# Up products that stream the high and the low part of x through one load of the high weights

## The chip, the cores and the metric

The kernel runs on one core of a Trainium2 chip. The metric is the device time of one execution in microseconds; before the change it is 268.32 us (median of three runs, 266.75 to 272.85).

## What is computed

A linear-attention recurrence over 768 steps (4 sequences, 8 heads of 48 channels) gives 3072 rows of 384 numbers, out. A mixture of experts then works on these rows: a row whose skip score is positive goes to the one of 8 experts with the largest gate logit.

```
def _moe_ref(x, w_skip, w_gate, w1, w2):
    out = x.copy()
    do_compute = x @ w_skip > 0
    xc = x[do_compute]
    e_idx = np.argmax(xc @ w_gate, axis=1)
    ...
    for e in range(E):                       # E = 8
        mask = e_idx == e
        h = np.maximum(xc[mask] @ w1[e], 0.0)        # up: 384 -> 1024
        y[mask] = gate_w[mask, None] * (h @ w2[e])   # down: 1024 -> 384
    out[do_compute] = xc + y
```

## The kernel before

The first 120 us or so compute the recurrence, write its rows to `out` in device memory, and build per expert a list of at most 232 rows (`CAP`). The change lies in what follows, the experts.

**Precision.** Products are made of numbers of a reduced kind, fp32r. Every operand is split in a high part, which is its rounded value, and a low part, which is what the rounding left. A product is the sum of three: high times high, low times high, high times low.

**Weights.** An expert's w1 and w2 are 6144 columns of 128 rows. They come in 12 pieces of 512 columns (`load_piece`, L106, issued on SP's queue). `split_piece` (L112) makes the parts: L115 on ScalarE casts a piece to its high part, L116 subtracts it from the raw piece, on VectorE or, for every third piece, on GpSimd. The pieces of expert e+1 are split while expert e computes. Raw pieces wait in `NST2` = 14 buffers; each split piece lets the next load start.

**One expert** (`expert`, L1009) works on its 232 rows in this order, which is the order of the instructions on every engine, since the program's order is kept there:

- Up (`up`, L155). The 1024 hidden features are eight slices of 128. A slice takes nine matmuls of 232 columns on TensorE: for each of three chunks of the 384 inputs the high weights with the high x, the high weights with the low x, the low weights with the high x, each with a weight load of its own, all into one PSUM region. Two slices share one PSUM bank; there are four banks of this kind (`banks`, L829: ps_p, ps_r, ps_l, ps_y).
- `rectify` (L163), once for a pair of slices: ScalarE writes the high part of the rectified sum, `hh` (L164), VectorE the low part, `hl` (L165), both straight from PSUM, 464 columns at once.
- `split_next(2)` after each pair splits two pieces of the next expert's weights, eight in the up phase.
- The next expert's rows are transposed (`turn`, L147): six transposes on TensorE, the high part xh on ScalarE (L152), the low part xl on VectorE (L153).
- Down (`down`, L167), for rows 0 to 127 and then 128 to 231: 24 matmuls of 384 columns, three for each slice, in the order of the slices: hh with the high w2, hh with the low w2, hl with the high w2. Two pieces are split behind each half, then `mix` (L173) on VectorE scales by the gate and adds x, and GpSimd scatters the rows to `out` (L178).

Expert 0 is done by other code (`single`), interleaved with the end of the recurrence and with the first two pairs of expert 1. Experts 2 and 3 have a few short VectorE instructions at their start (L1069 to L1086), which look for values out of range.

## Time and profile before

| what | value |
|---|---|
| median of three runs | 268.32 us |
| the profiled execution | 267.35 us |
| its span, from first to last instruction | 265.7 us |
| TensorE busy | 94% of the span |
| VectorE, ScalarE, GpSimd busy | 70%, 53%, 49% |
| experts 1 to 7 (up matmuls of expert 1 to the last mix) | 134.4 to 259.6 us |
| one full expert | 17.1 us |

The prediction shows rows of several views. A row of the chain of waits has a start, a length, the engine, the tile written, the line and a count. A row of a timeline has start, length, engine, line, operation, what is written and read, the sizes, and in brackets how long the engine had been idle and what ended that. A row by source line gives least, median and largest length in ns and the first and last start. In a row by groups stand total busy time, the mean in ns, and the idle time ahead. A window's row has the busy time of each engine. "PEld" are weight loads, which run beside the matmuls. Lines are those of the kernel before.

### The profile page before, as it was taken

The numbers are of one execution on the slowest core, as the hardware profiler recorded it, in microseconds if no ns is written. First come the engines' busy times: TensorE is split into PE (matmuls) and PEld (weight loads), VectorE is DVE, ScalarE is ACT, GpSimd is POOL, SyncE is SP. The second block draws the span as 40 slices with busy tenths as digits, with TensorE's granted clock in tenths as the row PEclk, the third lists the DMA queues.
The fourth block names the chain that finished last, engine by engine and source line by source line (L and its number), as shares of the span: only waits on it lengthen the run. The fifth ranks groups of instructions, "written<-read, shape, count | busy, mean of one in ns | idle before, by whom it ended". The sixth has DMA issues, their size and how long they took to land.

```text
span 265.7 us, 8819 instructions
## 1 busy us (share of the span) xinstructions
PE 249.5 (94%) x3593; PEld 229.1 (86%) x3594; DVE 187.3 (70%) x364; ACT 139.5 (53%) x314; POOL 130.9 (49%) x130
## 2 busy tenths in 40 slices
PE   7899888989999999899999999999999999999990
PEld 2689777877988989778799899999999999999990
DVE  7997446588989989786466996988478385692300
ACT  2556555656757667445377706648176282670200
POOL 8666233353728625502878837455535445345011
PEclk9999999999999999999999999999999999999997
DMA  6968788988899886449599797777738566001000
GB/s 196 292 191 265 210 239 266 275 273 266 246 260 280 238 276 179 104 119 317 164 326 277 248 323 259 219 233 243 251 110 259 171 205 218 20 1 46 0 35 21
DMA packets 31137, 53.92 MB, mean 203 GB/s; under 512 B 4603, under 2 KB 14471, under 8 KB 31088
## 3 DMA queue, kind: packets, MB, share of 16 engines
q1 hardware_dynamic: 28896, 48.09, 60.0%
q0 software_dynamic: 2048, 5.18, 6.2%
q8 instruction: 30, 0.49, 0.8%
q14 instruction: 19, 0.16, 0.2%
q10 hardware_dynamic: 144, 0.00, 0.0%
HBM read 45.46 MB, written 8.39 MB: 203 GB/s over the span
## 4 chain that ended last, share of the span: by engine, by line
PE 71%; DVE 18%; DMA 4%; issue 3%; ACT 1%; SPq 0%; POOL 0%; POOLq 0%; DVEq 0%
PE ps_p L170 11%; PE ps_y L170 11%; PE ps_p L446 6%; PE ps_p L160 5%; PE ps_r L160 5%; PE ps_l L160 5%; PE ps_y L160 5%; PE ps_y L508 5%; DVE am L467 3%; PE ps_s L479 3%; DVE am L468 3%; DVE rd L416 2%; PE ps_l L459 2%; DVE rd L424 2%; PE ps_y L532 2%
## 5 line engine op out<-in xcount | busy, mean ns | idle before, releaser
L116 POOL TENSOR_TENSOR lo<-raw,hi 128x512 fp32r<-128x512 f32 x40 | 54.1, 1355 | 59.7 <-ACT hi L115 48.6
L115 ACT CAST hi<-raw 128x512 fp32r<-128x512 f32 x96 | 54.7, 623 | 0.0
L116 DVE TENSOR_TENSOR lo<-raw,hi 128x512 fp32r<-128x512 f32 x56 | 50.7, 930 | 2.5 <-ACT hi L115 1.9
L434 POOL TENSOR_TENSOR kd<-dm,w_d 128x512 f32<-128x512 f32 x23 | 31.6, 1382 | 15.4 <-DMA dm<-in_dm_dram 8.3
L178 POOL DMA_INDIRECT out_dram<-xg,sid x16 | 17.3, 1079 | 36.3 <-DVE xg L175 28.5
L467 DVE COPY_PREDICATED am<-below,ps_p 128x512 f32<-128x512 int8 x24 | 17.7, 738 | 17.6 <-PE ps_p L446 17.5
L446 PE MATMUL ps_p<-rd,kd 64*64 64x128 f32 x768 | 27.3, 276 | 0.8 <-issue 0.8
L128 POOL DMA_INDIRECT xg<-out_dram,gid x16 | 18.4, 1151 | 16.8 <-DMA raw<-in_w_dram 10.8
L446 PEld LDWEIGHTS ps_p<-rd,kd 64*64 64x64 f32 x768 | 21.0, 132 | 4.5 <-issue 2.4
L508 PE MATMUL ps_y<-vz,am 128*64 128x96 f32 x384 | 20.6, 248 | 3.9 <-DVE am L468 1.6
L164 ACT ACTIVATE hh<-ps_p 128x464 fp32r<-128x464 f32 x7 | 3.9, 559 | 37.6 <-PE ps_p L160 22.9
L410 ACT ACTIVATE rd<-rd,uw 128x128 f32<-128x128 f32 x50 | 17.2, 395 | 9.6 <-DVE rd L416 9.6
L508 PEld LDWEIGHTS ps_y<-vz,am 128*64 128x64 f32 x384 | 17.4, 137 | 5.2 <-ACT xT L576 1.9
L479 PE MATMUL ps_s<-vz,kt 128*64 128x96 f32 x352 | 19.6, 252 | 0.9 <-issue 0.9
L461 ACT COPY kt<-ps_l 128x512 f32<-128x512 f32 x22 | 12.9, 585 | 13.0 <-PE ps_l L459 12.8
L170 PE MATMUL ps_p<-hi,hh 128*128 128x384 f32 x56 | 19.4, 347 | 0.0
L170 PE MATMUL ps_p<-hi,hl 128*128 128x384 f32 x56 | 19.0, 340 | 0.4 <-issue 0.4
L479 PEld LDWEIGHTS ps_s<-vz,kt 128*64 128x64 f32 x352 | 15.3, 136 | 4.3 <-issue 4.2
L170 PE MATMUL ps_y<-hi,hh 128*104 128x384 f32 x56 | 18.9, 338 | 0.0
L170 PE MATMUL ps_y<-lo,hh 128*104 128x384 f32 x56 | 18.9, 337 | 0.0
L170 PE MATMUL ps_y<-hi,hl 128*104 128x384 f32 x56 | 18.9, 337 | 0.0
L170 PE MATMUL ps_p<-lo,hh 128*128 128x384 f32 x56 | 18.8, 336 | 0.0
(239 smaller groups left out, 670.3 us busy)
## 6 DMA issues: line engine op xcount, KB each, us to landing
raw<-in_w_dram SPq DMA_DIRECT2D x96, 256.0 KB
dm<-in_dm_dram SPq DMA_DIRECT2D x24, 512.0 KB
vz<-in_tok_dram SPq DMA_DIRECT2D x48, 96.0 KB
out_dram<-xt SPq DMA_DIRECT2D x48, 96.0 KB
out_dram<-xt SPq DMA_DIRECT2D x4, 192.0 KB
xg<-out_dram,gid POOLq DMA_INDIRECT x16
out_dram<-xg,sid POOLq DMA_INDIRECT x16
wgp<-in_wgq_dram SPq DMA_DIRECT2D x1, 96.0 KB
```

The costliest lines, as they stand in the source:

```text
L115: nc.scalar.copy(hi, t)
L116: eng.tensor_tensor(lo, t, hi.bitcast(F32), ALU.subtract)
L128: ins = nc.gpsimd.indirect_dma_start(out=xg[:m], out_offset=None, in_=out[0:rows], in_offset=bass.IndirectOffsetOnAxis(ap=gid[:m, q : q + ...
L160: nc.tensor.matmul(ph, a[:, c, fs], b[:, c, :], start=(k == 0), stop=(k == 3 * NCC - 1))
L170: nc.tensor.matmul(py, a, b[:, f, :], start=(k == 0), stop=(k == 3 * NFC - 1))
L178: ins = nc.gpsimd.indirect_dma_start(out=out, out_offset=bass.IndirectOffsetOnAxis(ap=sid[: listed(q), q : q + 1], axis=0), in_=xs.pop(q)[ ...
L410: nc.scalar.mul(rd[:, :, 1], rd[:, :, 0], uw[:, hp : hp + 1])
L434: (eng or nc.gpsimd).tensor_tensor(kds[n], d[:, 1], w_d[:, n % NSUB, 1][:, :, None].to_broadcast([DR, NHP, 2, C]), ALU.mult,)
L446: nc.tensor.matmul(ps_p[q * C : (q + 1) * C, a, 2 * hp * C : 2 * (hp + 1) * C], kd[h, hp, q, :], rd[h, hp, q].rearrange("p s c -> p (s c)" ...
L467: nc.vector.copy_predicated(shape(am[n % 2]), below, p[:, :, 0])
L479: nc.tensor.matmul(s[a * C : (a + 1) * C, :, hp * D : (hp + 1) * D], kt[:, hp, a, :], t[:, :, a, hp, :], start=i == 0 and hp == 0, stop=Tr ...
L508: ins = nc.tensor.matmul(place_y(a, c)[:, :, g, :], am[n % 2][:, a, hp * C : (hp + 1) * C], t[:, :, a, hp, :], start=g == 0 and n % NSTEP ...
```

## The change

`x` of an expert becomes one tile with the high and the low part side by side. For each chunk, one matmul moves both, 464 columns, past one load of the high weights, into a whole PSUM bank: the first 232 columns hold high times high, the last 232 hold low times high. A second matmul of 232 columns adds the low weights times the high x to the first half. So a slice takes six matmuls and six weight loads instead of nine, with the same number of columns in all, and it takes a whole PSUM bank; the four banks go round twice in an expert.

Since the sum now lies in two halves, `rectify` is called for each slice, and makes it of four instructions of 232 columns: ScalarE copies the second half to `h` in SBUF, VectorE adds the first half to it, ScalarE writes the rectified high part from `h`, VectorE the low part from `h`. `h` has three buffers. `NST2` falls from 14 to 12, and while expert 1 runs, GpSimd takes three of twelve low parts of weights instead of two.

```
--- before.py
+++ after.py
-NST2 = 14
+NST2 = 12
...
-    def up(ph, w1, f, xh, xl):
+    def up(ph, w1, f, x):
         fs = slice(f * P, (f + 1) * P)
-        k = 0
         for c in range(NCC):
-            for a, b in ((w1[0], xh), (w1[0], xl), (w1[1], xh)):
-                nc.tensor.matmul(ph, a[:, c, fs], b[:, c, :], start=(k == 0), stop=(k == 3 * NCC - 1))
-                k += 1
-
-    def rectify(ph, hh, hl):
-        nc.scalar.activation(hh, ph, AF.Relu)
-        nc.vector.scalar_tensor_tensor(hl, ph, 0.0, hh.bitcast(F32), ALU.max, ALU.subtract)
+            nc.tensor.matmul(
+                ph.rearrange("p s q -> p (s q)"),
+                w1[0][:, c, fs],
+                x[:, c].rearrange("p s q -> p (s q)"),
+                start=(c == 0),
+                stop=(c == NCC - 1),
+                skip_group_check=True,
+            )
+            nc.tensor.matmul(
+                ph[:, 0, :], w1[1][:, c, fs], x[:, c, 0, :], start=False, stop=(c == NCC - 1), skip_group_check=True
+            )
+
+    def rectify(ph, h, hh, hl):
+        nc.scalar.copy(h, ph[:, 1, :])
+        nc.vector.tensor_tensor(h, ph[:, 0, :], h, ALU.add)
+        nc.scalar.activation(hh, h, AF.Relu)
+        nc.vector.scalar_tensor_tensor(hl, h, 0.0, hh.bitcast(F32), ALU.max, ALU.subtract)
...
-                        split_piece(e, j, nc.gpsimd if j % (6 if e == 2 else 3) == 2 else nc.vector)
+                        split_piece(e, j, nc.gpsimd if j % (4 if e == 2 else 3) == 2 else nc.vector)
...
-                turned[e] = tuple(
-                    w2pool.tile([P, NCC, CAP], F32R, tag="x" + t, name=f"x{t}{e}") for t in ("h", "l")
-                )
-            xh, xl = turned[e]
+                turned[e] = w2pool.tile([P, NCC, 2, CAP], F32R, tag="x", name=f"x{e}")
+            x = turned[e]
...
             for f0 in range(0, NFC, 2):
-                ph = bank("ph")[:, : 2 * CAP].rearrange("p (i q) -> p i q", q=CAP)
-                for i in range(2):
-                    up(ph[:, i, :], w1, f0 + i, xh, xl)
-                rectify(ph, hh[:, f0 : f0 + 2, :], hl[:, f0 : f0 + 2, :])
+                for f in (f0, f0 + 1):
+                    ph = bank("ph")[:, : 2 * CAP].rearrange("p (s q) -> p s q", q=CAP)
+                    up(ph, w1, f, x)
+                    h = w2pool.tile([P, CAP], F32, tag="h", name=f"h{e}_{f}", bufs=3)
+                    rectify(ph, h, hh[:, f, :], hl[:, f, :])
                 yield
                 split_next(2)
```

How it moves instructions, on VectorE, in the up phase of expert 4. Before (hl and hh are the low and high part of the hidden features, lo, raw and hi those of a weight piece, the number in a raw's name is the piece's):

```order
L165 SCALAR_TENSOR_TENSOR hl_3268<-ps_p,hh_3267 128x464
L116 TENSOR_TENSOR lo_89<-raw_0_3050,hi_87 128x512
L116 TENSOR_TENSOR lo_89<-raw_1_3054,hi_87 128x512
L165 SCALAR_TENSOR_TENSOR hl_3268<-ps_r,hh_3267 128x464
L116 TENSOR_TENSOR lo_89<-raw_3_3097,hi_87 128x512
L165 SCALAR_TENSOR_TENSOR hl_3268<-ps_l,hh_3267 128x464
L116 TENSOR_TENSOR lo_89<-raw_4_3121,hi_87 128x512
```

With the change, the same place, as far as piece 3:

```order
L172 TENSOR_TENSOR h_0_3291<-ps_p,h_0_3291 128x232
L174 SCALAR_TENSOR_TENSOR hl_3284<-h_0_3291,hh_3283 128x232
L172 TENSOR_TENSOR h_1_3302<-ps_r,h_1_3302 128x232
L174 SCALAR_TENSOR_TENSOR hl_3284<-h_1_3302,hh_3283 128x232
L116 TENSOR_TENSOR lo_89<-raw_0_3104,hi_87 128x512
L116 TENSOR_TENSOR lo_89<-raw_1_3108,hi_87 128x512
L172 TENSOR_TENSOR h_2_3321<-ps_l,h_2_3321 128x232
L174 SCALAR_TENSOR_TENSOR hl_3284<-h_2_3321,hh_3283 128x232
L172 TENSOR_TENSOR h_3_3332<-ps_y,h_3_3332 128x232
L174 SCALAR_TENSOR_TENSOR hl_3284<-h_3_3332,hh_3283 128x232
L116 TENSOR_TENSOR lo_89<-raw_3_3138,hi_87 128x512
```

Where one instruction stood for a pair of slices there are four; each L174 reads an hh that ScalarE makes from the h of the L172 ahead of it. The pieces of weights stand where they stood, between the pairs.

On ScalarE, the same place. Before:

```order
L164 ACTIVATE hh_3267<-ps_p 128x464
L115 CAST hi_87<-raw_0_3050 128x512
L115 CAST hi_87<-raw_1_3054 128x512
L164 ACTIVATE hh_3267<-ps_r 128x464
L115 CAST hi_87<-raw_2_3093 128x512
```

With the change:

```order
L171 COPY h_0_3291<-ps_p 128x232
L173 ACTIVATE hh_3283<-h_0_3291 128x232
L171 COPY h_1_3302<-ps_r 128x232
L173 ACTIVATE hh_3283<-h_1_3302 128x232
L115 CAST hi_87<-raw_0_3104 128x512
L115 CAST hi_87<-raw_1_3108 128x512
L171 COPY h_2_3321<-ps_l 128x232
L173 ACTIVATE hh_3283<-h_2_3321 128x232
```

The copy of slice 1 stands behind the Relu of slice 0 (L173), which waits for VectorE's add; the casts of the weight pieces stand behind the Relu of slice 1.

More of the change, by code (lines that the diff above doesn't have):

```diff
@@ L997, in turn_one @@
             if j == 0:
-                turned[e] = tuple(
-                    w2pool.tile([P, NCC, CAP], F32R, tag="x" + t, name=f"x{t}{e}") for t in ("h", "l")
-                )
-            xh, xl = turned[e]
+                turned[e] = w2pool.tile([P, NCC, 2, CAP], F32R, tag="x", name=f"x{e}")
+            x = turned[e]
             c = TILES[j][1]
-            turn(bank("pt")[:, :DM].rearrange("p (c q) -> p c q", q=P), j * E + e, xh[:, :, c], xl[:, :, c])
+            turn(bank("pt")[:, :DM].rearrange("p (c q) -> p c q", q=P), j * E + e, x[:, :, 0, c], x[:, :, 1, c])
         def turn_all(e):
@@ L1007, in turn_all, with expert @@
                 turn_one(e, j)
-        def expert(e, xh, xl):
+        def expert(e, x):
             w1, w2 = views(e)
@@ L1057, in tile_wkv_moe @@
             elif c == "u":
-                opened = opened or expert(1, *turned.pop(1))
+                opened = opened or expert(1, turned.pop(1))
                 next(opened)
@@ L1086, in tile_wkv_moe @@
                 nc.vector.tensor_copy(flags[:, 1:2], lmin[:, 0:1])
-            both(opened if e == 1 else expert(e, *turned.pop(e)))
+            both(opened if e == 1 else expert(e, turned.pop(e)))
     any_v = nc.values_load(flags[0:1, 1:2], min_val=0, max_val=1)
```

## The prediction

> **What bounds the kernel now.** I read the page first, then the chain of waits, then the stages by windows, and last the timelines of VectorE (DVE) and ScalarE (ACT) inside one expert. The changed code runs once for each of experts 1 to 7, so it is one expert's period that has to be costed.
>
> ```profile
> span 265.7 us, 8819 instructions
> PE 249.5 (94%) x3593; PEld 229.1 (86%) x3594; DVE 187.3 (70%) x364; ACT 139.5 (53%) x314; POOL 130.9 (49%) x130
> ```
>
> From the chain, expert 6 and the first rows of expert 7:
>
> ```profile
> 225.41 2.01 PE ps_p L160 x18
> 227.42 2.02 PE ps_r L160 x18
> 229.44 2.01 PE ps_l L160 x18
> 231.46 2.01 PE ps_y L160 x18
> 233.46 0.33 PE ps_t L151 x3
> 233.79 0.27 PE ps_s L151 x3
> 234.06 4.22 PE ps_p L170 x24
> 238.28 4.20 PE ps_y L170 x24
> 242.48 2.01 PE ps_p L160 x18
> ```
>
> This stage is TensorE and nothing else: four up groups, 8.04 us, six transposes for the next expert, 0.60, and two down groups, 8.42, joined without a gap; one period is 242.48 − 225.41 = 17.07 us. By windows (columns: PE, PEld, DVE, ACT, POOL busy, then clock, DMA share, GB/s) the expert before it and the last one are:
>
> ```profile
> 208.35:225.41 17.06, 17.06 (x128) 16.89 (x128) 10.92 (x16) 9.12 (x18) 7.75 (x6) 1.00 0.60 193
> 242.48:258.98 16.50, 16.46 (x120) 15.95 (x119) 3.81 (x7) 2.24 (x4) 2.02 (x2) 1.00 0.07 21
> ```
>
> The granted clock is 1.00. VectorE has some 6 us of every period free and ScalarE 8, and the other engines' waits do not appear in the chain at all. So a gain on TensorE counts fully, as long as VectorE and ScalarE go on delivering in time. Whether they do is the question here.
>
> **What TensorE saves.** 18 matmuls of 232 columns take 2.01 us, 0.112 each; 24 of 384 columns take 4.20, 0.175 each. One wider form stands in the trace:
>
> ```profile
> 133.26 0.39 PE L200 MATMUL ps_y<-hi,xhl 128*128 128x512 f32 x1
> 133.49 0.40 PE L200 MATMUL ps_y<-lo,xhl 128*128 128x512 f32 x1
> ```
>
> That is 0.23 from start to start for 512 columns. The three lie on one line, about 15 ns plus 0.42 ns a column, so 464 columns cost 0.209. A slice of 128 hidden features (one f) takes 9 × 0.112 = 1.005 us now and 3 × (0.209 + 0.112) = 0.963 then: the columns stay, three fixed parts of 15 ns go. Eight slices take 7.70 instead of 8.04: 0.34 us an expert, 2.4 us for seven.
>
> **What VectorE and ScalarE get.** Now a pair of slices leaves PSUM in two wide instructions, one on each engine. Afterwards each slice needs four in a row, changing engine each time: copy (ACT), add (DVE), Relu (ACT), low part (DVE). Today's pattern, from expert 5:
>
> ```profile
> 210.08 0.28 PE L160 MATMUL ps_p<-xh,lo 128*128 128x232 f32 x1
> 210.44 0.56 ACT L164 ACTIVATE hh<-ps_p 128x464 fp32r<-128x464 f32 x1 [6.71 <-issue]
> 210.90 1.13 ACT L115 CAST hi<-raw 128x512 fp32r<-128x512 f32 x2
> 211.03 0.64 DVE L165 SCALAR_TENSOR_TENSOR hl<-ps_p,hh 128x464 fp32r<-128x464 f32 x1 [2.03 <-ACT hh L164]
> 211.59 1.28 DVE L116 TENSOR_TENSOR lo<-raw,hi 128x512 fp32r<-128x512 f32 x2
> 213.57 1.29 POOL L116 TENSOR_TENSOR lo<-raw,hi 128x512 fp32r<-128x512 f32 x1 [3.24 <-ACT hi L115]
> 214.03 1.38 DVE L116 TENSOR_TENSOR lo<-raw,hi 128x512 fp32r<-128x512 f32 x1 [0.38 <-ACT hi L115]
> ```
>
> Four prices come out of these rows. ScalarE starts 0.36 after the issue of the last up matmul (210.08 to 210.44). A result of ScalarE is used by VectorE 0.03 later (211.00 to 211.03). An instruction that waits for nothing starts 0.08 (DVE, 211.67 against 211.59) or 0.10 (ACT) before the end of the one ahead. And a piece of 512 on VectorE, 0.68 alone, takes 1.38 when GpSimd is in the middle of its own: it ends 0.55 after GpSimd's end (214.86 to 215.41).
>
> No instruction of 232 elements stands in the trace. The nearest rows:
>
> ```profile
> L204 ACT ACTIVATE h<-ps_p x2: 378/382/386, 119.9 to 120.2; 128x256 f32<-128x256 f32 x2
> L659 ACT ACTIVATE df<-df x4: 231/245/260, 55.4 to 119.0; 128x64 f32<-128x64 f32 x2, 128x32 f32<-128x32 f32 x2
> L115 ACT CAST hi<-raw 128x512 fp32r<-128x512 f32 x48 | 26.9, 623 | 0.0
> 218.29 0.43 ACT L152 CAST xh<-ps_s 128x312 fp32r<-128x312 f32 x1
> 219.25 0.47 DVE L153 TENSOR_TENSOR xl<-ps_s,xh 128x312 fp32r<-128x312 f32 x1
> L424 DVE TENSOR_TENSOR rd<-rd,uw x23: 411/425/1407, 6.0 to 107.2; 128x256 f32<-128x256 f32 x23
> L116 DVE TENSOR_TENSOR lo<-raw,hi x56: 674/683/4141, 129.6 to 238.8; 128x512 fp32r<-128x512 f32 x56
> ```
>
> By straight lines through two sizes: copy from PSUM 0.365 (464: 0.56, 312: 0.43); add with one PSUM source 0.385 (464: 0.64, 312: 0.47); Relu from SBUF 0.39 (64: 0.26, 512: 0.62); low part with two SBUF sources 0.40 (256: 0.425, 512: 0.683). From below they cannot cost less than half the 464 rows (0.28, 0.32), from above not more than the 256, 312 and 512 rows. I take the lines, which the 256 rows support.
>
> **One expert after the change**, counted from its first up matmul. Both engines work in order, and the two are locked to each other: behind VectorE's wait for the Relu stand the next add, the weight pieces and the mix of the output; behind ScalarE's wait for the add stand the next copy and the casts.
>
> - Slice 0: its last matmul is issued at 0.85, copy 1.21 to 1.58, add to 1.99, Relu to 2.41.
> - From one Relu's end to the next within a pair: the low part starts 0.03 later, the add 0.32 after that, and ends 0.385 on, 0.03, Relu 0.39: 1.155. TensorE delivers a slice every 0.963. Four such steps: 4.62.
> - From a pair to the next, two weight pieces stand between. Pieces 0 and 1 both on VectorE: the two casts end 1.03 after the Relu, VectorE's second piece ends its turn at 1.75, add and Relu follow: 2.56. Pieces 2 (GpSimd) and 3 (VectorE): GpSimd runs 0.60 to 1.90, VectorE's piece ends 0.55 after it: 3.20. Pieces 4 (VectorE) and 5 (GpSimd): 2.14, and the low part of slice 6 then has GpSimd ahead of it, 0.30: 2.44.
> - The last low part: 0.43.
>
> Sum: 2.41 + 4.62 + 2.56 + 3.20 + 2.44 + 0.43 = 15.66. TensorE wants that low part much sooner. Its up phase is 7.70, plus 0.20 because slice 7 reuses the PSUM bank of slice 3, whose add ends at 6.86; transposes 0.60; 23 of the first down group's 24 matmuls 4.03: it is wanted at 12.53. The stall is 15.66 + 0.08 − 12.53 = 3.21 us, inside the first down group. The period becomes 7.90 + 0.60 + 4.20 + 3.21 + 4.20 = 20.11, against 17.07: **+3.04 for an expert**, its 0.34 already taken off. Today there is room:
>
> ```profile
> 217.02 0.64 DVE L165 SCALAR_TENSOR_TENSOR hl<-ps_y,hh 128x464 fp32r<-128x464 f32 x1 [0.47 <-ACT hh L164]
> ```
>
> Expert 5's last low part is ready at 217.66, and wanted 4.0 us into the 8.42 of the down phase that ends at 225.41, at 221.0.
>
> Experts 2 and 3 begin with extra work on VectorE:
>
> ```profile
> 158.27 0.26 DVE L1069 TENSOR_SCALAR lok<-lg 128x216 f32<-128x216 f32 x1
> 159.48 0.16 DVE L1075 CAST bad<-lmin 128x1 bf16<-128x1 f32 x1
> 174.65 1.18 DVE L1081 TENSOR_TENSOR redo<-cnt 128x1 f32<-128x1 f32 x1
> 176.50 0.15 DVE L1086 CAST flags<-lmin 128x1 int32<-128x1 f32 x1
> ```
>
> The first add would be due 1.61 after the stage's start, at 158.6 and 175.7, but VectorE is free only at 159.6 and 176.6: +1.0 and +0.9. Today's slack takes that up, a locked chain does not. Expert 7 splits no weights and turns nothing: its last low part comes at 2.41 + 7 × 1.155 + 0.43 = 10.9, wanted at 11.7: no stall, −0.34. Expert 1 shares its up phase with the second half of expert 0; I give it the same +3.04.
>
> Total: 6 × 3.04 + 1.0 + 0.9 − 0.34 = +19.8. Against the profiled execution's 267.35 (span 265.7 and 1.65 around it) that is **287 us**. The median of the three runs shown, 268.32, is 1.0 above that execution, so a median may come out at 288.
>
> **What I cost at nothing.** Twelve buffers for raw pieces instead of 14: the casts of pieces (the L115 row above) waited 0.0 us, and twelve buffers still hold one whole expert ahead, with periods that get longer. If that cover went, each piece would cost its load: ten took 9.2 us, 0.92 each.
>
> ```profile
> 212.30 9.22 SPq L110 DMA_DIRECT2D raw<-in_w_dram  x10
> ```
>
> The other share of pieces for GpSimd in expert 1 (three of twelve instead of two) moves 0.6 us from VectorE to GpSimd there; inside expert 1's stall it is within my error.
>
> [...]
>
> **Rivals.**
>
> *The work hides, TensorE keeps its gain.* By busy time there is room: VectorE's 10.92 plus 16 × 0.39 − 4 × 0.64 is 14.6, ScalarE's 9.12 plus 16 × 0.38 − 4 × 0.56 is 13.0, both below 17. Then 267.35 − 2.4 = 265.0, not slower than before. It decides if the last low part comes by 12.5 instead of 15.7, so if each of the seven steps were 0.45 shorter; a step inside a pair would be 0.7, less than one add and one Relu. What speaks against it is the order of the work, not its amount.
>
> *Cheaper small instructions.* If the four cost half of the 464 rows, steps inside a pair take 0.95, the three longer ones 0.15 less, slice 0 is 0.2 earlier: 1.45 less per expert. 6 × 1.6 + 1.9 − 0.3 gives 278.5. The rows of 64 and 256 elements, with their visible fixed part, speak against it.
>
> *Dearer hand-overs.* There are four where there was one. At 0.10 each instead of 0.03, an expert loses 1.4 more: 6 × 4.4 + 1.6, 295. With every price at its upper row it would be about 303. The 0.03 row speaks against it; expert 1's already crowded VectorE speaks for it.
>
> **How the numbers follow.** My forecast, the locked chain with a loss of 2.2 to 4 us an expert (282 to 293), 0.62; cheaper instructions, 274 to 282, 0.17; dearer ones, over 293, 0.12; the work hides, 0.09. The range is 276 to 297: the first case with most of the second and third; the 303 end lies outside, since it needs all four prices at their worst. Two per cent (5.4 us) is about what a measurement of this kernel can tell. The case that hides gains 0.9% at most, so it counts as within 2%: 0.08 with the tail of the cheap case. Faster by over 2%: 0.02, for what I do not see. Slower: 0.90.
>
> **What would show it.** Right: expert periods of 19.5 to 21 us, the last at 16.2; a TensorE gap before late down matmuls of slices 5 to 7, released by VectorE; copies, adds and Relus alternating on the two engines with each mostly waiting for the other; up matmuls at 0.209 and 0.112. Wrong: periods at 16.7 with no gap, or copies that run ahead of the chain, or 232-element instructions well under 0.3.

## The result and the profile after

| what | before | after |
|---|---|---|
| median | 268.32 us (three runs) | 289.97 us (four runs, 289.4 to 291.34) |
| the profiled execution, its span | 267.35, 265.7 us | 289.78, 288.0 us |
| ratio after to before | | 1.085, 95% interval 1.076 to 1.093 |

A fourth run of the kernel before took 1356.81 us; it stands apart from all others and is not in the ratio. Ratios, here and below, compare only the runs within 1.5% of the fastest of their kernel (here without the 272.85 of the kernel before), so they don't always follow from the medians, and the profiles of e9, e10, e12 and e13 are of longer runs than these. The change makes the kernel slower by 8.5%. The prediction said 287.0 us, 276 to 297.

The head of the page, after:

```profile
span 288.0 us, 8670 instructions
PE 257.0 (89%) x3425; PEld 224.0 (78%) x3426; DVE 210.6 (73%) x447; ACT 160.8 (56%) x398; POOL 131.8 (46%) x131
```

TensorE falls from 94% to 89% of a longer span. VectorE is busy 23.3 us more and ScalarE 21.3, yet VectorE's share rises by only three points: neither became full.

An expert's period is read here from the start of one last mix (the one of 104 rows) to the start of the next, on the timeline of VectorE:

```profile
225.21 0.60 DVE L184 SCALAR_TENSOR_TENSOR xg<-ps_y,gate_s,xg 104x384 f32<-104x384 f32 x1
245.26 0.60 DVE L184 SCALAR_TENSOR_TENSOR xg<-ps_y,gate_s,xg 104x384 f32<-104x384 f32 x1
```

The mix of expert 4 and that of expert 5: 20.05 us. All experts, in both kernels:

| | expert 1's last mix at | period of expert 2 | 3 | 4 | 5 | 6 | 7 |
|---|---|---|---|---|---|---|---|
| before | 157.74 | 16.38 | 17.20 | 17.06 | 17.07 | 17.07 | 16.46 |
| after | 161.16 | 22.25 | 21.72 | 20.08 | 20.05 | 20.01 | 16.06 |
| difference | 3.42 | 5.87 | 4.52 | 3.02 | 2.98 | 2.94 | −0.40 |

The differences add up to 22.35 us, the whole difference of the two spans (22.3). The last expert, which splits no weights, got faster.

A mix can come late behind TensorE, and that shifts time from one column to the next. In the kernel before, expert 1's last mix stands behind two weight pieces of VectorE's and starts 0.90 after expert 2's first up matmul (156.84), where the last mixes of experts 3 to 6 start 0.20 after the next expert's. So the 16.38 of expert 2 is not a shorter expert: from first up matmul to first up matmul expert 2 takes 17.12 before and 22.41 after, and expert 1 ends 3.95 later (160.79 against 156.84).

The windows of experts 4, 5 and 7 (span of the window, then busy time of PE, PEld, DVE, ACT and POOL, then clock, DMA share, GB/s):

```profile
205.13:225.21 20.08, 18.12 (x104) 15.93 (x103) 14.48 (x29) 12.14 (x30) 7.44 (x7) 1.00 0.56 172
225.21:245.26 20.05, 18.11 (x104) 15.94 (x103) 14.46 (x30) 12.13 (x30) 7.40 (x7) 1.00 0.56 173
265.27:281.33 16.06, 16.02 (x96) 14.99 (x94) 7.00 (x19) 5.21 (x16) 4.28 (x4) 1.00 0.10 33
```

In expert 4 before, TensorE was busy 17.06 of 17.06; now 18.12 of 20.08, at a granted clock of 1.00. VectorE has 5.6 us free in each period and ScalarE 7.9, and still TensorE waits for them. The chain of waits in expert 5 shows why:

```profile
232.22 1.13 ACT hi L115 x2
233.38 1.35 DVE lo L116
234.73 0.32 DVE h L172
235.08 0.41 ACT hh L173
235.51 0.40 DVE hl L174
235.91 0.32 DVE h L172
236.36 0.20 issue
236.56 1.13 ACT hi L115 x2
237.68 0.26 ACT h L171
237.96 0.41 DVE h L172
238.40 0.41 ACT hh L173
238.82 0.47 DVE hl L174
239.29 0.32 DVE h L172
239.64 0.41 ACT hh L173
```

Where the chain before read TensorE from end to end, it now leaves TensorE at the end of the up product and changes between ScalarE and VectorE eight times in these rows, through the four instructions of each slice and the weight pieces between the pairs. It comes back to TensorE only for the last matmuls of the first down group. TensorE's own waits there, from its timeline:

```profile
235.10 0.44 PE L179 MATMUL ps_p<-hi,hh 128*128 128x384 f32 x1 [1.32 <-DVE h L172]
238.84 0.44 PE L179 MATMUL ps_p<-hi,hh 128*128 128x384 f32 x1 [0.32 <-ACT hh L173]
240.09 0.44 PE L179 MATMUL ps_p<-hi,hh 128*128 128x384 f32 x1 [0.29 <-ACT hh L173]
240.80 0.34 PE L179 MATMUL ps_y<-hi,hh 128*104 128x384 f32 x1
```

The first, the seventh and the eighth slice's first down matmul wait. The first down group runs from 235.10 to 240.80, 5.70 us, where it took 4.22 before.

### The profile page after: what moved, and what is told of

Its sections match the earlier page's. It is cut to its first block, busy times and chain, and to the rows that moved or that the text cites. A ratio compares the mean times of both kernels' runs of the same rounds, so it can differ in the third digit from the quotient of the medians.

```text
span 288.0 us, 8670 instructions
## 1 busy us (share of the span) xinstructions
PE 257.0 (89%) x3425; PEld 224.0 (78%) x3426; DVE 210.6 (73%) x447; ACT 160.8 (56%) x398; POOL 131.8 (46%) x131
## 4 chain that ended last, share of the span: by engine, by line
PE 33%; DVE 24%; ACT 9%; issue 6%; DMA 5%; SPq 1%; POOL 0%; POOLq 0%; ACTq 0%; DVEq 0%
PE ps_y L179 7%; DVE lo L116 6%; ACT hi L115 5%; DVE h L172 4%; DMA raw<-in_w_dram 3%; ACT hh L173 3%; DVE hl L174 3%; PE ps_p L179 3%; PE ps_p L455 3%; PE ps_y L517 2%; PE ps_l L158 2%; PE ps_p L158 2%; PE ps_r L158 2%; DVE am L476 2%; DMA xg<-out_dram,gid 2%
## 5 line engine op out<-in xcount | busy, mean ns | idle before, releaser
L116 DVE TENSOR_TENSOR lo<-raw,hi 128x512 fp32r<-128x512 f32 x55 | 46.2, 863 | 6.5 <-ACT hi L115 3.5
L173 ACT ACTIVATE hh<-h 128x232 fp32r<-128x232 f32 x56 | 22.3, 397 | 43.5 <-DVE h L172 38.3
L174 DVE SCALAR_TENSOR_TENSOR hl<-h,hh 128x232 fp32r<-128x232 f32 x56 | 24.1, 431 | 25.9 <-ACT hh L173 23.6
L179 PE MATMUL ps_p<-hi,hh 128*128 128x384 f32 x56 | 21.4, 383 | 11.2 <-DVE h L172 7.3
L187 POOL DMA_INDIRECT out_dram<-xg,sid x16 | 17.9, 1122 | 26.1 <-DVE xg L184 13.8
L455 PEld LDWEIGHTS ps_p<-rd,kd 64*64 64x64 f32 x768 | 21.3, 132 | 5.1 <-issue 3.0
L179 PEld LDWEIGHTS ps_p<-hi,hh 128*128 128x128 f32 x56 | 10.9, 195 | 16.1 <-DVE h L172 8.5
L425 DVE TENSOR_TENSOR rd<-dm,w_d 128x512 f32<-128x512 f32 x24 | 21.4, 892 | 0.2 <-DMA dm<-in_dm_dram 0.2
L179 PE MATMUL ps_p<-hi,hl 128*128 128x384 f32 x56 | 20.7, 370 | 0.0
L470 ACT COPY kt<-ps_l 128x512 f32<-128x512 f32 x22 | 12.9, 585 | 13.6 <-PE ps_l L468 13.5
L179 PE MATMUL ps_p<-lo,hh 128*128 128x384 f32 x56 | 19.5, 348 | 0.0
```

The lines of the kernel that those rows point to most:

```text
L116: eng.tensor_tensor(lo, t, hi.bitcast(F32), ALU.subtract)
L173: nc.scalar.activation(hh, h, AF.Relu)
L174: nc.vector.scalar_tensor_tensor(hl, h, 0.0, hh.bitcast(F32), ALU.max, ALU.subtract)
L179: nc.tensor.matmul(py, a, b[:, f, :], start=(k == 0), stop=(k == 3 * NFC - 1))
L425: nc.vector.tensor_tensor(rds[n][:, :, :, 0], d[:, 0], w_d[:, n % NSUB, 0][:, :, None].to_broadcast([DR, NHP, 2, C]), ALU.mult,)
L455: nc.tensor.matmul(ps_p[q * C : (q + 1) * C, a, 2 * hp * C : 2 * (hp + 1) * C], kd[h, hp, q, :], rd[h, hp, q].rearrange("p s c -> p (s c)" ...
```

## The experiments

Periods and times of all of them, in one place. "Mix 1" is the start of expert 1's last mix in the profile; ratios are against runs of the kernel before on the same chip.

| run | mix 1 | 2 | 3 | 4 | 5 | 6 | 7 | median us | ratio (95%) |
|---|---|---|---|---|---|---|---|---|---|
| e1_pair | 161.09 | 22.97 | 17.70 | 17.60 | 17.59 | 17.62 | 16.14 | 278.51 | 1.035 (1.026 to 1.044) |
| e2_no_low_x | 158.12 | 17.29 | 16.68 | 16.77 | 16.77 | 16.77 | 16.14 | 268.59 | 0.998 (0.991 to 1.004) |
| e3_no_tie | 163.16 | 22.93 | 21.50 | 20.08 | 21.09 | 20.09 | 16.09 | 294.28 | 1.096 (1.086 to 1.107) |
| e4_side_edits | 160.41 | 17.08 | 17.20 | 17.06 | 17.07 | 17.07 | 16.46 | 270.01 | 1.005 (1.000 to 1.010) |
| e5_no_pieces | 168.61 | 23.63 | 16.87 | 16.78 | 16.77 | 16.77 | 16.14 | 283.96 (one run) | |
| e6_pieces_moved | 160.45 | 20.94 | 21.50 | 19.77 | 19.75 | 19.77 | 16.15 | 287.43 | 1.066 (1.056 to 1.076) |
| e7_pairs_and_pieces | 160.94 | 18.10 | 17.95 | 16.49 | 16.77 | 16.77 | 16.14 | 270.76 | 1.011 (1.005 to 1.017) |
| e8_one_behind | 161.08 | 17.51 | 17.97 | 16.15 | 16.77 | 16.78 | 16.14 | 272.24 | 1.015 (1.006 to 1.024) |
| e9_expert3_pieces | 165.26 | 21.96 | 20.08 | 20.03 | 20.02 | 20.04 | 16.08 | 291.0 | 1.077 (1.067 to 1.087) |
| e10_sum_in_psum | 162.05 | 16.77 | 18.35 | 16.77 | 16.78 | 16.77 | 16.14 | 272.07 | 1.007 (1.001 to 1.012) |
| e12_no_holdups | 162.70 | 16.76 | 16.86 | 16.77 | 16.76 | 16.77 | 16.14 | 270.86 | 1.002 (0.997 to 1.007) |
| e13_early_unit | 164.30 | 17.77 | 16.86 | 16.76 | 16.77 | 16.76 | 16.14 | 270.98 | 1.009 (1.005 to 1.013) |

The periods of experts 4 to 6 agree with one another to 0.1 us in all runs but e3, e7 and e8 (in e7 and e8 only expert 4's mix column stands out, since expert 3's last mix was late; TensorE takes 16.77 or 16.78 from expert to expert), so they tell theories apart where the total, with up to 5 us between one run of the kernel before and another (265.8 to 271.0), does not.

### e1_pair: the same instructions in another order

```
-    rectify(ph, h, hh[:, f, :], hl[:, f, :])      # copy, add, Relu, low part of a slice
+    join(ph, h)                                   # copy, add; then, behind the pair's second:
+    for f, h in zip((f0, f0 + 1), hs):
+        rectify(h, hh[:, f, :], hl[:, f, :])      # Relu, low part
```

Expected:

> The same instructions as in the changed kernel, only their order within a pair of slices is another: both copies and both adds first, then both Relus and both low parts. Locked chain (mine): VectorE no longer stands still while ScalarE does the Relu of the same slice, because the next slice's add is in between; a pair then takes some 0.7 us less from its first add to its last low part, four pairs 2.5 to 3, and most of the stall in the first down group goes. Periods of experts 4 to 6 of 17.3 to 17.9 instead of 20.05, total 274 to 277. Rival (the amount of work on VectorE and ScalarE sets the time): no instruction less, so 289 to 291. Rival (the wait for a PSUM bank at the start of the down phase sets the time): no change either.

Measured: experts 4 to 6 take 17.6, in the range of the theory; 2.4 us of the 3.0 that each had lost are back, with no instruction less. VectorE in expert 5:

```profile
227.79 0.39 DVE L172 TENSOR_TENSOR h<-ps_p,h 128x232 f32<-128x232 f32 x1
228.10 0.38 DVE L172 TENSOR_TENSOR h<-ps_r,h 128x232 f32<-128x232 f32 x1
228.64 0.71 DVE L176 SCALAR_TENSOR_TENSOR hl<-h,hh 128x232 fp32r<-128x232 f32 x2 [0.16 <-ACT hh L175]
```

A pair now costs VectorE one idle spell of 0.16 in place of two of 0.46: while ScalarE makes the first Relu, VectorE does the second add. The total missed its range by 1.5 us. Expert 2 took 22.97 where expert 3 took 17.70: in it a piece of weights took 3.75 on VectorE while GpSimd did two of its own (172.26 to 174.76), TensorE waited 3.50 for what stood behind it, and its next matmuls ran at a clock of 0.50. Such hold-ups are taken up in e9 and e10.

### e2_no_low_x and e3_no_tie: without the chain, and without the wait for the bank's other half

```
 e2: -    nc.scalar.copy(h, ph[:, 1, :])
     -    nc.vector.tensor_tensor(h, ph[:, 0, :], h, ALU.add)
     +    # Relu and low part read ph[:, 0, :]
 e3: +    tc.declare_no_dep(down_matmul, add)      # in short: the last 8 adds; the last part of expert 0 too
```

> The matmuls of the changed kernel, but the second half of the sum (high weights times low x) is computed and then left out: no copy, no add; Relu and low part straight from PSUM, one slice at a time. So TensorE has the new work and the two other engines have no chain of four. Mine: no stall, TensorE keeps its 0.34 us an expert: periods of 16.7, total 264.5 to 265.5 on the scale of 267.4 for the kernel before (ratio 0.99). Rival (wider matmuls save nothing, or the new PSUM banks cost on their own): 267 or more. Rival (64 instructions more on the two engines already stall TensorE, whatever the order): over 270.

> The changed kernel without one wait: the first down matmul, in one half of the two-bank tile ps_p, no longer waits for the add of slice 4, which reads the other half (the same for ps_y and the last part of expert 0). Locked chain (mine): the last low part sets the end, so the gap of 1.4 us at the start of the down phase only moves to slices 5 to 7: periods of experts 4 to 6 stay at 19.9 to 20.1; expert 1 may gain up to 1.6; total 288 to 290. Rival (this bank wait is the cost): 1.4 less an expert, 280 to 282.

Measured: without copy and add an expert takes 16.77, so what TensorE saves is real: 17.07 − 16.77 = 0.30 each. The total can't be told from that of the kernel before; it missed the expected 0.99, and what the periods gained did not show in it.

The wait of 1.32 in e3: the down product writes the other half of the two-bank tile ps_p whose first half slice 4 uses, and the program keeps the two apart as one tile. Without that dependency experts 4 and 6 take 20.08 and 20.09, as before it. The stall only moves, to one place at slice 6 (timeline of TensorE, expert 5):

```profile
239.12 0.45 PE L182 MATMUL ps_p<-hi,hh 128*128 128x384 f32 x1 [0.15 <-ACT hh L176]
241.27 0.44 PE L182 MATMUL ps_p<-hi,hh 128*128 128x384 f32 x1 [1.26 <-ACT hh L176]
```

So the wait is a symptom: whoever waits earlier waits less later, since the last low part sets the end. That the total of e3 is even 4.3 us above the change's has two parts in the profile: a later start of the stage (2.0 at expert 1's last mix, all of it there already at expert 1's first up matmul, 136.71 against 134.56) and stretches at a lower clock (expert 5's 21.09; 0.58 from 241.2 to 245.0). Why they come was not tried.

### e4_side_edits: the two side edits alone, on the kernel before

```
-NST2 = 14
+NST2 = 12
-    nc.gpsimd if j % (6 if e == 2 else 3) == 2 else nc.vector
+    nc.gpsimd if j % (4 if e == 2 else 3) == 2 else nc.vector
```

> The kernel before with the two side edits alone: twelve raw buffers instead of 14, and GpSimd takes three instead of two low parts of expert 2's weights. Mine: nothing, 267 to 268.5, ratio 1.00. Rival (shorter look-ahead of the weight loads makes casts wait): over 270, with casts waiting for loads.

Measured: 270.01 against 268.52, above the expected 268.5, with an interval that just takes in 1. The periods from expert 3 on are those of the kernel before to 0.01. But in the profile TensorE gets to expert 2 3.37 later (160.21 against 156.84), and all of that arises in expert 1, whose first up matmul comes at 134.44 (before 134.42). A piece of GpSimd runs there from 150.61 to 151.90, where in the kernel before one ran from 152.17, and two pieces of VectorE's beside it take 3.10 instead of 1.28. The low part behind them comes late, and TensorE waits for it:

```profile
153.66 0.44 PE L170 MATMUL ps_p<-hi,hl 128*128 128x384 f32 x1 [2.24 <-DVE hl L165]
```

Casts waited for loads 2.2 us in all, in three places (in the kernel before nowhere), but all before 110 us, and the first up matmul came no later for it; the rival's wait was there and cost nothing. So the side edits are not quite the nothing that they were taken for: in this one profile expert 1 ends 3.37 later with them, where with the whole change it ends 3.95 later.

### e5_no_pieces: the chain alone

```
-    if j is not None:
+    if j is not None and e > 3 and j < 8:
+        raw.pop((e, j)); load_next(1)
+    elif j is not None:
```

> The changed kernel without pieces 0 to 7 of the weights of experts 4 to 7: they are neither cast nor given a low part (so the results of those experts come from stale parts, a part of the work that is left out), and in experts 3 to 6 nothing stands on VectorE and GpSimd between the pairs of the up product. What is left is the four small instructions of each slice in the order of the change, with 1.17 us from slice to slice where nothing stands between them, against 0.963 of TensorE. Theory (the locked order together with the pieces between the pairs makes the stall): the last low part then comes 2.4 + 7 x 1.17 + 0.4 = 11.0 us after the start of the up product and is wanted at 12.5, so the stall of the first down group goes away and experts 4 to 6 take 16.6 to 16.9 us instead of 20.0. Rival (the locked order of four is by itself enough: with three banks TensorE is held to 1.17 a slice, since the pieces cost only their own time): 8 x (1.17 - 0.963) = 1.7 more, 18.3 to 18.6.

Measured: 16.87, 16.78, 16.77, 16.77 for experts 3 to 6, with TensorE never waiting in expert 5. The rival is out: a step of 1.17 is longer than TensorE's 0.963, but with four banks for eight slices and 4 us of down matmuls ahead of the last low part, the chain has room. VectorE in expert 5:

```profile
227.29 0.40 DVE L172 TENSOR_TENSOR h<-ps_p,h 128x232 f32<-128x232 f32 x1 [0.78 <-ACT h L171]
228.15 0.40 DVE L174 SCALAR_TENSOR_TENSOR hl<-h,hh 128x232 fp32r<-128x232 f32 x1 [0.46 <-ACT hh L173]
228.47 0.39 DVE L172 TENSOR_TENSOR h<-ps_r,h 128x232 f32<-128x232 f32 x1
...
236.38 0.40 DVE L174 SCALAR_TENSOR_TENSOR hl<-h,hh 128x232 fp32r<-128x232 f32 x1 [0.46 <-ACT hh L173]
```

The add of one slice stands 1.18 behind that of the slice ahead, and the last low part ends at 236.78, 9.1 us after the first add's end; in the changed kernel 13.5 (226.96 to 240.46). The locked order alone costs TensorE nothing here, and the pieces alone, in the kernel before, did not either: it takes both.

### e6, e7 and e8: pieces moved, then the order as well

```
 all three:  after a pair     -    split_next(2)      +    split_next(1)
             after a down half -   split_next(2)      +    split_next(4)
 e7: with the order of e1
 e8: +    join(ph, h)
     +    if f:
     +        rectify(last, hh[:, f - 1, :], hl[:, f - 1, :])
     +    last = h
     ...                                  # the last slice's at the end of the last pair
```

> The changed kernel with its order of small instructions, one weight piece instead of two after each pair of slices and four instead of two behind each half of the down product; all the work is done. Theory (the chain of the small instructions has to end before the down product wants it, and what stands behind the down halves has to end before the mixes and the next expert's first copy): the up product's slices get 4 pieces out of their way, but eight pieces stand behind the down halves, about 2.0 us more on VectorE there, and hold up the mix and the start of the next expert; the two nearly cancel, experts 4 to 6 take 19.5 to 20.3, total 286 to 291. Rival (only the pieces between the pairs count): the last low part comes 2 x 0.7 + 2 x 0.7 = about 2.8 earlier, experts 4 to 6 take 17.0 to 17.5 and the total is 268 to 272.

> The small instructions ordered by pairs (copy, add, copy, add, then Relu, low part, Relu, low part), which brought experts 4 to 6 to 17.6, together with the moved pieces (one after each pair, four behind each down half); all the work is done. Theory of the locked chain: with the order by pairs a hand-over of one engine lies under the other's work, so that the late pieces are taken up in the down product: experts 4 to 6 take 16.7 to 17.2, total 267 to 272 with expert 2 at 17 to 22. Rival (the pieces behind the down halves hold up the next expert as much as they help this one): 17.5 or more.

> The Relu and the low part of a slice are issued behind the copy and the add of the next slice (the last slice's at the end of the last pair), and the pieces moved as in the run by pairs; all the work is done. Theory of the locked chain: no engine waits for the other's last instruction, so a slice costs VectorE 0.39 + 0.40 and ScalarE 0.35 + 0.40, both under TensorE's 0.963; experts 4 to 6 take 16.6 to 16.9 like the run without the low part of x, total 264 to 269, no stall above 0.5 at the first down group; below the kernel before by up to 2 us if expert 2 keeps to 17. Rival (expert 2's GpSimd pieces and the half clock cost what they did in the changed kernel, whatever the order): experts 4 to 6 as said, but expert 2 at 22 to 23 and the total 271 to 275.

Measured: moving the pieces alone gives back 0.3 of 3.0 (19.77). In their new place they hold up the mix, for which TensorE waits 0.5 at the start of the next expert, and one of GpSimd's holds that expert's first low part, 1.63 long. The rival is out. With the order by pairs and the pieces moved, and with the order one behind, experts 5 and 6 take 16.77, as if copy and add were not there. All four small instructions of every slice are done, and they cost TensorE nothing. So "the work hides", the rival of the prediction that it rightly held unlikely for this kernel, is true of another order of the same work. The order one behind was not run with the pieces left in their place, so its share is not known by itself; for the order by pairs it is 2.4 of the 3.0 (e1). The totals are 1.1 and 1.5% above the kernel before, e7's in its range, e8's above it (264 to 269). For e8 that is where the rival had it (272.24), though not for its reason: expert 2 takes 17.51 and not 22. Experts 2 and 3 together lose some 2 us, and expert 1 ends 3.3 later than in the kernel before, 1.9 of it being there at its first up matmul (136.28 against 134.42).

### e9 and e10: what experts 2 and 3 cost more

In the changed kernel, three instructions of VectorE took far longer than their kind. From the timeline of VectorE and GpSimd in that kernel, the middle of expert 2's up product and the start of expert 3:

```profile
169.71 1.30 POOL L116 TENSOR_TENSOR lo<-raw,hi 128x512 fp32r<-128x512 f32 x1
169.78 1.79 DVE L116 TENSOR_TENSOR lo<-raw,hi 128x512 fp32r<-128x512 f32 x1 [0.62 <-issue]
172.34 1.72 DVE L174 SCALAR_TENSOR_TENSOR hl<-h,hh 128x232 fp32r<-128x232 f32 x1 [0.47 <-ACT hh L173]
172.48 1.32 POOL L116 TENSOR_TENSOR lo<-raw,hi 128x512 fp32r<-128x512 f32 x1
183.93 1.78 DVE L1089 TENSOR_TENSOR redo<-cnt 128x1 f32<-128x1 f32 x1
184.38 1.30 POOL L116 TENSOR_TENSOR lo<-raw,hi 128x512 fp32r<-128x512 f32 x1
```

Each overlaps a piece of GpSimd and ends 0.03 to 0.56 after it, even an addition of a single column (0.15 elsewhere). All three have both operands in SBUF.

```
 e9:  -    nc.gpsimd if j % (4 if e == 2 else 3) == 2 else nc.vector
      +    nc.gpsimd if j % (4 if e == 2 else 3) == 2 and e != 3 else nc.vector
 e10: (on e8)
      -    nc.vector.tensor_tensor(h, ph[:, 0, :], h, ALU.add)
      +    nc.vector.tensor_tensor(ph[:, 0, :], ph[:, 0, :], h, ALU.add)
      -    last = h
      +    last = ph[:, 0, :]
```

> The changed kernel, all of its work, with one difference: the low parts of expert 3's weights, which are made while expert 2 is computed, all go to VectorE (four of the twelve stood on GpSimd). Theory (what experts 2 and 3 cost beyond the 20.0 of experts 4 to 6 is three instructions of VectorE with two operands in SBUF that stood still behind GpSimd's pieces: 1.79 instead of 0.68, 1.72 instead of 0.40 and 1.78 instead of 0.15): expert 2 goes from 22.25 to 20.0 to 20.9 and expert 3 from 21.72 to 20.0 to 20.5; experts 4 to 6 stay at 20.0; total 286 to 288. Rival (the half clock after the gap in expert 2, or its scatters, make the excess): expert 2 stays at 21.8 to 22.5, total 289 to 291.

> The run one behind (Relu and low part issued behind the next slice's add, pieces moved), all of its work, with one difference: the add writes its sum back to the bank of the product, so that Relu and low part read it there and the low part has one operand in SBUF instead of two. Theory (GpSimd holds only VectorE's instructions with two operands in SBUF): no low part takes longer than 0.5, where the run one behind had 1.0 in each expert and 1.98 and 1.76 in expert 2; expert 2 goes from 17.5 to 16.8 to 17.2, experts 4 to 6 stay at 16.77, expert 3 keeps its 17.5 to 18.0 (its hold-up is another instruction, 2.42); total about 0.5 to 1 below the run one behind. Rival (the bank is now free only behind the low part, a slice later, and TensorE waits for it): experts 4 to 6 at 17.2 to 18.

Measured in e9: expert 3 goes to 20.08, as expected, but expert 2 stays at 21.96, where the rival had it. The timeline of e9 tells why the rival is not thereby right:

```profile
172.84 1.92 DVE L174 SCALAR_TENSOR_TENSOR hl<-h,hh 128x232 fp32r<-128x232 f32 x1 [0.46 <-ACT hh L173]
173.20 1.29 POOL L116 TENSOR_TENSOR lo<-raw,hi 128x512 fp32r<-128x512 f32 x1
187.74 0.15 DVE L1089 TENSOR_TENSOR redo<-cnt 128x1 f32<-128x1 f32 x1
```

One piece was left on GpSimd, the eleventh of expert 2's own weights, which the side edit (4 in place of 6) puts there, behind three scatters; a low part met it. My experiment had not taken away all that it meant to. This hold-up (1.92 for 0.40) and the few instructions at the expert's start (0.46, see below) make up the 1.9 by which expert 2 still exceeds a steady one, so nothing is left there for the half clock or the scatters. The additions at the start of expert 3 are back at 0.15. The total, 1.077, can't be told from the change's 1.085. In the profile expert 1 ended 4.1 us later than in the changed kernel; all of that is there at its first up matmul (138.66 against 134.56), ahead of anything that this edit touches, and one profile doesn't show why.

e10 is the clean test: the low part, with 56 instructions in each kernel (least, median and largest length in ns), first in e8, with both operands in SBUF, then in e10, with one of them in PSUM:

```profile
L176 DVE SCALAR_TENSOR_TENSOR hl<-h,hh x56: 383/391/1982, 139.2 to 255.2; 128x232 fp32r<-128x232 f32 x56
```

```profile
L176 DVE SCALAR_TENSOR_TENSOR hl<-ps_p,hh x14: 379/389/399, 140.2 to 254.1; 128x232 fp32r<-128x232 f32 x14
L176 DVE SCALAR_TENSOR_TENSOR hl<-ps_l,hh x14: 386/389/391, 144.6 to 256.0; 128x232 fp32r<-128x232 f32 x14
```

Not one is held any more (the other two banks' largest are 0.392 and 0.400), and expert 2 takes 16.77, exactly the period of the undisturbed experts, instead of 17.51. That is not for want of a meeting: eight low parts of e10 overlap a piece of GpSimd, and all take 0.39 to 0.40, such as this one:

```profile
237.82 1.28 POOL L116 TENSOR_TENSOR lo<-raw,hi 128x512 fp32r<-128x512 f32 x1 [3.84 <-SPq L1107]
238.33 0.39 DVE L176 SCALAR_TENSOR_TENSOR hl<-ps_r,hh 128x232 fp32r<-128x232 f32 x1
```

Expert 3 keeps a hold-up, in which an addition of one column took 2.12; its 18.35 lies above the expected 17.5 to 18.0. The total is 0.7% above the kernel before, where e8 had 1.5%, but the two intervals overlap.

### e12 and e13: towards a version that beats the kernel before

```
 e12: (on e10)
      -    nc.vector.tensor_tensor(redo, cnt[:, 0:1], cnt[:, 1:2], ALU.add)
      +    nc.vector.tensor_tensor(redo, pb[:, 0:1], cnt[:, 1:2], ALU.add)   # pb: in PSUM
      ...
      -NST2 = 12        +NST2 = 13        -bufs=3        +bufs=2   # of h
      -    j % (4 if e == 2 else 3)        +    j % (6 if e == 2 else 3)
 e13: (on e12) the second "u" of PLAN taken out
```

> The run with the sum in PSUM, all of its work, with the two additions at the start of expert 3 reading their first operand in PSUM instead of a copy in SBUF (one of them took 2.12 instead of 0.15 behind GpSimd's pieces), one buffer more for the weight pieces, one less for the copies, and expert 2's pieces on GpSimd as in the kernel before. Theory (these two-operand instructions are the last hold-up behind GpSimd on the way to the up product): expert 3 goes from 18.35 to 16.8 to 17.1, the others stay at 16.77 and 16.14; from expert 1's last mix to expert 7's 100.0 to 100.4, against 101.2 in the kernel before; total 266 to 270, by how late expert 1 ends. Rival (another wait stands behind the one removed, VectorE's other pieces): expert 3 at 17.5 to 18.4.

> The run without hold-ups, all of its work, with the second early unit of expert 1's up product (its slices 2 and 3, issued ahead of expert 0's last part) moved behind that part; slice 3 shares its bank with that part, which waited 0.94 to 2.63 for slice 3's add in the kernels with an add. Theory (that wait is what expert 1 loses): expert 1's last mix comes 1 to 2.5 earlier, at 158 to 160, total 265 to 268. Rival (TensorE has the wait for expert 0's gather or hidden parts to fill there anyway, so the unit is only missing elsewhere): expert 1's last mix at 160.5 to 163, total the same or up to 2 more.

A version between e10 and e12 (e11: 14 raw buffers as before the change, and expert 3's pieces all on VectorE) gave no time: a pool of it wanted 72.56 KB of SBUF per partition, and 69.94 were left. Hence the 13 buffers and the two for `h` in e12.

Measured in e12: expert 3 takes 16.86. VectorE's row there, which lies inside two pieces of GpSimd's (178.94 to 181.48), and the window of expert 2:

```profile
179.99 0.14 DVE L1096 TENSOR_TENSOR redo<-ps_s,cnt 128x1 f32<-128x1 f32 x1
```

```profile
163.00:180.00 17.00, 17.00 (x105) 16.07 (x105) 15.18 (x36) 11.88 (x31) 11.02 (x9) 1.00 0.68 218
```

TensorE is busy throughout again, as before the change, with VectorE at 15.2 of 17. From expert 1's last mix to expert 7's it is 100.06 us, against 101.24 in the kernel before: 1.2 us are won; counted from expert 2's first up matmul it is 1.9 (100.26 against 102.14), about six times the 0.30 of e2. The total is not: 1.002, 0.997 to 1.007, no difference from the kernel before. In the profile expert 1 ends at 162.70 against 157.74, with 3.5 of these 5.0 us there at its first up matmul (137.93 against 134.42).

e13 took one suspected cause of that away and won nothing: expert 0's last mix comes earlier (144.72 against 148.10), but its TensorE then waits elsewhere, and expert 1 takes 19.58 from there instead of 14.60. Its last mix, at 164.30, lies above the ranges of theory and rival; the total, 270.98 against e12's 270.86, is where the rival had it. From its timeline and its window of that stretch:

```profile
150.50 0.48 PE L158 MATMUL ps_r<-x,hi 128*128 128x464 f32 x1 [2.92 <-DVE hl L176]
```

```profile
147.00:163.00 16.00, 13.08 (x70) 12.25 (x69) 13.82 (x28) 9.60 (x24) 7.98 (x8) 0.89 0.75 226
```

The unit of expert 1 that is done early fills TensorE's time there, as the rival said. No version here beats the kernel before.

## Why the prediction was right

**The mechanism is the one predicted, and the experiments bear it out.** Two in-order engines that hand each slice to and fro, with weight pieces between: undoing the lock gives most of the periods back (e1), taking the chain away (e2) or the pieces (e5) all of it, and with the work unchanged another order together with another place for half of the up phase's pieces does as well (e7, e8). The rival by amounts of work had the amounts about right, 14.6 and 13.0 against 14.5 and 12.1 measured, and the wrong conclusion for this order.

**The terms, one by one:**

| term | predicted | measured |
|---|---|---|
| copy, add, Relu, low part | 0.365, 0.385, 0.39, 0.40 | 0.33 to 0.35, 0.39, 0.397, 0.401 |
| slice on TensorE | 0.963 | 0.96 to 0.97 |
| step inside a pair | 1.155 | 1.17 |
| steps between pairs | 2.56, 3.20, 2.44 | 2.58, 3.16, 2.15 |
| last low part after the first up matmul | 15.66 | 15.50 (224.96 to 240.46) |
| waits inside the up phase | 0.20 | 0.35 |
| stall at the first down group | 3.21 | 2.99 (1.49 ahead of it, 1.50 inside) |
| period | 20.11 | 20.01 to 20.08 |
| expert 7 | −0.34 | −0.40 |

The prices stand in the rows by line of the changed kernel:

```profile
L173 ACT ACTIVATE hh<-h x56: 396/397/399, 136.5 to 275.2; 128x232 fp32r<-128x232 f32 x56
L174 DVE SCALAR_TENSOR_TENSOR hl<-h,hh x56: 399/401/1720, 137.0 to 275.7; 128x232 fp32r<-128x232 f32 x56
L172 DVE TENSOR_TENSOR h<-ps_r,h x14: 388/393/395, 137.3 to 272.5; 128x232 f32<-128x232 f32 x14
```

Straight lines through two other sizes gave all four prices to within 0.035, and a step inside a pair took 1.17, where hand-overs of 0.10 each would have made it some 1.3; so the rivals "cheaper" and "dearer" fell. ("Cheaper" was summed with a step of 0.95. With halves of the rows of 464 columns the step is 0.90, and that rival's total would have been some 276 instead of 278.5; no forecast hangs on it.) The steps are the distances of the Relus' ends in expert 5. The stall is counted against the transposes' end (233.01 + 0.60): the first down matmul comes at 235.10, 1.49 late, and its group takes 5.70 instead of 4.20.

**Where the prediction was off:**

- *The third step between pairs*: "the low part of slice 6 then has GpSimd ahead of it, 0.30". No run shows that 0.30, an estimate of mine; the hold-up cost 0.07: 0.47 instead of 0.40, and the step to that slice came out at 2.15.
- *The place of the stall*: it was put inside the first down group; half of it stands ahead of the group, as the wait for slice 4's add that e3 looked into, and behind it TensorE was released by ScalarE's Relus, not by VectorE as the prediction's sign had it. It changed nothing in the sum.
- *Experts 2 and 3, "+1.0 and +0.9"*: the mis-sized terms. Expert 2 cost 2.2 more than a steady expert, expert 3 1.67 more. In expert 2, the few instructions at its start cost 0.46 (the first add comes 1.81 behind the mix, in expert 5 1.35), and the two hold-ups by GpSimd the rest: from add to add, the step ahead of slice 4 is 3.60 (3.17 in expert 5) and the next 2.50 (1.16). In expert 3 it is the one-column addition, 1.78 instead of 0.15, and e9 shows that its other five cost next to nothing. I had read that row before the change (1.18) as extra work, and it was already a hold-up: it ended at 175.83, and a piece of GpSimd's at 175.81.
- *Expert 1, "the same +3.04"*: 3.95 came out, and that it is so near is in part luck. TensorE's waits there are not the stall of a steady expert: 2.17 of them stand in expert 0's last part, which waits for slice 3's add, and only 1.27 in expert 1's first down group. And e4, without copy and add, ended expert 1 3.37 late: the moved share of GpSimd's pieces, put at nothing in the prediction, may have made part of it.
- *The sum*, 19.8 against 22.35, came out 2.5 short. Counted from first up matmul to first up matmul, 1.25 of that is expert 2 (5.29 for 4.04), 0.61 expert 3 (4.55 for 3.94) and 0.91 expert 1 (3.95 for 3.04), less 0.2 by which experts 4 to 6 were cheaper. The base of 17.07 for each expert before was right.

**GpSimd beside VectorE.** The low part took up to 1.98 with both operands in SBUF (e8) and never more than 0.400 with one in PSUM (e10), beside pieces of GpSimd's in both. I had put the hold-up at 0.30 for an expert; it was 0.07 in a steady one and 1.8 in expert 2.

**What stays open**: why expert 1 ends later, by 2.0 to 8.0 us (at expert 2's first up matmul), in all profiles of kernels with the copy and add (11.4 in e5's single run), even when its successors run without a stall. Two parts can be told apart. One lies ahead of expert 1's first up matmul, which came at 134.42 in the kernel before, at 134.56 in the changed one, and at 136.3 to 138.7 in e1, e3, e8, e9, e10, e12 and e13, though the code up to there differs in little but the number of raw buffers. What moves it was not tried, and it may be no more than what sets one run of a kernel apart from another. The other part lies between that matmul and expert 2's: 22.42 before, 23.2 to 24.6 in e1, e6, e8, e10 and e12, and 26.23 in the changed kernel; but it is 25.77 in e4, which has neither copy nor add. So what the chain itself costs expert 1 is not shown. In nearly all of these kernels expert 0's last part waits for an add of slice 3 of expert 1, whose bank shares a tile with its own, 0.9 to 2.6 us; e13 moved that wait and did not win.

## What to carry to other kernels

Ask of an added instruction not only what it costs but whose answer it waits for: four short instructions that alternate between two in-order engines cost 1.17 us where either engine works only 0.8 of them, and everything that stands between them, useful as it is, is added to the chain. Before giving up such a change, issue the second half of one tile behind the first half of the next; here that, with half of the weight pieces between the tiles moved to a later place, made 3 us an expert vanish with the same instructions. And where GpSimd works beside VectorE, give VectorE's urgent instructions an operand in PSUM if there is a choice: beside a piece of GpSimd's a one-column addition took 0.14 so (e12), and up to 2.42 with both in SBUF (e8).

## What the hardware showed that I had not expected

In expert 2 of the changed kernel TensorE's clock fell after the wait of 1.76 ahead of the first down group. Windows of the changed kernel, the first of them behind an even longer wait (2.17, ended at 143.29):

```profile
143.30:146.50 3.20, 3.20 (x19) 3.12 (x20) 1.22 (x3) 3.20 (x7) 2.71 (x3) 1.00 0.81 266
170.00:173.00 3.00, 1.24 (x8) 1.07 (x7) 2.54 (x3) 0.71 (x2) 2.80 (x3) 1.00 0.45 140
173.00:176.40 3.40, 3.40 (x14) 3.37 (x12) 2.75 (x5) 1.67 (x4) 1.28 (x2) 0.56 0.87 275
```

Down matmuls then start 0.32 apart instead of 0.175, for 3 us. It cost that expert nothing, since slice 6's Relu came only at 176.95 and its matmul waited for it anyway. In e1 a gap of 3.50 was followed by a clock of 0.50 (176.1 to 181.0); here it was one of 1.76, with 0.56 behind it. The gap of 2.17 in the changed kernel was not followed by a lower clock (1.00 in the first window). In e3, gaps of 1.26 or 1.27 were, in three experts: 0.56 from 180.0 to 183.4 (expert 2), 0.66 from 199.9 to 203.0 (expert 3), 0.58 from 241.2 to 245.0 (expert 5); in its experts 4 and 6, with TensorE idle for 1.71 of 20 us (207 to 227, 249 to 269), the clock was 1.00. What decides among gaps of 1.2 to 2.2 us remains open, but these show that it isn't their length alone; behind the three of e3 the down matmuls started 0.32 apart instead of 0.175 for 2.2 to 3.2 us.
